# A gated recurrence and a feed-forward block: one reference point per sequence in place of six levels per block

## The chip, the core and the metric

The kernel runs on one core of one Trainium2 chip. The metric is the device time of one execution in microseconds (us). The core has five engines that work side by side, each through a queue of its own and in that queue's order: TensorE (PE in the profile; its weight loads stand apart as PEld), VectorE (DVE), ScalarE (ACT), GpSimd (POOL) and SyncE (SP), whose queue issues the DMAs. Matmuls write to PSUM, which has 8 banks; the other data lies in SBUF, on 128 partitions.

## What is computed

There are 4 sequences of 768 steps, 8 heads and 48 dimensions per head. Each head keeps a complex 48x48 state that is multiplied at every step by a complex gate per row and takes up the outer product of key and value; the query reads its real part. The result, 3072 tokens of 384 features, goes through a feed-forward block with 2048 hidden units and Silu.

```python
    mag = np.sqrt(a_re * a_re + a_im * a_im)
    scale = np.minimum(mag, 0.999) / (mag + 1e-06)
    a_re_n, a_im_n = (a_re * scale, a_im * scale)
    for t in range(S):
        ar, ai = (a_re_n[:, :, t, :, None], a_im_n[:, :, t, :, None])
        new_re = ar * S_re - ai * S_im
        new_im = ar * S_im + ai * S_re
        kv = np.einsum('bhd,bhe->bhde', k[:, :, t], v[:, :, t])
        S_re, S_im = (new_re + kv, new_im)
        y[:, :, t] = np.einsum('bhd,bhde->bhe', q[:, :, t], S_re)
    ...
    h = x @ w_in
    g = h * (1.0 / (1.0 + np.exp(-h)))
    return (g @ w_out).astype(np.float32)
```

The inputs are drawn with `a_re = rand * 0.1 + 0.85` and `a_im = randn * 0.1`. All arrays are float32 but the two weight matrices, which arrive as float64 and are turned into float32 on the chip.

## The kernel before

A sequence is cut into 6 chunks of 128 steps; the 24 chunks go in 12 pairs, and 256 tokens, a pair, are a tile of the feed-forward block. The kernel writes a gate as exp(l + 2 pi i th), forms running sums of l and th, and gets the weight between two steps as a product of rotated and scaled keys and queries.

*Gates of a pair* (`gates_log`, `gates_angle`): a chain that alternates ACT (squares, Ln, Exp, Arctan under two function tables), DVE and POOL. `phases` (L278, L280) sums th with two matmuls a chunk and `trig` takes cosine and sine. POOL rotates keys and queries (`rotate`, L306).

*Scales*: so that no exponent grows, a chunk is split into two blocks of 64 steps and each pair of steps takes its reference from the middle of the smallest aligned run that holds both. `scales` makes six sums of l for each head with two 128x384 matmuls (L341, tile `lt`) and ACT takes exponentials of them (tile `z`); `scaled` multiplies keys and queries by these on DVE (L357); `weights` forms the weights as three overlapping products (`far`, `mid`, `near`, L401 to L410) that DVE merges by masks (L416 to L418). `key_state` (L315, L320) scales keys to the end of their block, and `state` (L383, L387, L390) carries the state from block to block on PE, POOL and DVE.

*Output* (L424, L428) gives y with the tokens on partitions, so `tokens` (L442) transposes it for the feed-forward block.

*Feed-forward*: 8 units per pair. `hidden` (L450, tile `h`) forms 256 hidden units with 6 matmuls, ACT takes Tanh and DVE forms h(1 + tanh(h/2)) (L455); `result` (L465, tile `o`) adds them into two PSUM banks with 4 matmuls. `load_w` (L125 to L146) turns a block of float64 weights into float32 with nine DVE operations on 24 blocks of 256 and 32 of 192 columns.

*Order*: the code merges the steps of the attention of pair p with the feed-forward steps of pair p - 1, and with the weight loads at p = 0. The framework then puts each engine's instructions in one fixed queue and gives PSUM tiles out of small pools: `p_a` has 3 banks for the attention, `p_h` has 1 and `p_o` has 2 for the feed-forward.

Of the kernel before, what the change touches and what calls it, by code (L numbers as in the profile page):

```python
# [11 lines left out]
I32 = mybir.dt.int32  # L12
AF = mybir.ActivationFunctionType
# [4 lines left out]
# Square of the smallest gate magnitude that is told from zero: such a gate passes on 2e-9 of  # L18
# the state, less than fp32 rounds off, and keeps the exponents of a run of 4 within +-41.
FLOOR2 = 2.07e-15  # L20
# Adding and taking away 1.5 * 2^23 rounds an fp32 number to an integer.
ROUND = 12582912.0
# The largest fp32 number under 2 pi, so that half a turn stays within the sine's range.
TWO_PI = 6.283185


@with_exitstack
def kernel(
# [11 lines left out]
    """The gated recurrence in blocks of 64 steps, with the state carried from block to block.  # L40

    A gate is exp(l + 2 pi i th). With L and TH the running sums of l and th, step s reaches step t
    with the weight sum_d q[t,d] k[s,d] exp(L[t]-L[s]) cos(TH[t]-TH[s]): a product of rotated
    queries and keys, (q cos, q sin) and (k cos, k sin), each scaled by the distance of its L from
    one between. For any two steps of a block that one is the middle of the smallest aligned run
    of 8, 16, 32 or 64 steps that holds them in different halves (levels w = 4 to 32), so that both
    scales are at most 1 however fast the gates decay; steps of the same run of 4 take its middle,
    at most 2 steps away. Chunks of 128 steps, two blocks, fill the partitions.
    """
# [66 lines left out]
    def load_w(dst, src):  # L116
        """float64, as 64-bit words, to the nearest float32: sign, exponent and 23 bits of the
        mantissa are put together from the bits, and the other 29 bits are added. Columns that
        come in float32 are taken as they are."""
# [23 lines left out]
        # Below 2^-126 the exponent doesn't fit: such a weight is zero in float32.  # L143
# [11 lines left out]
    make_identity(nc, ident)  # L155

    def triangle(t, w):
        """1 where s <= t and both are in one aligned run of w steps."""
        nc.gpsimd.memset(t, 1.0)
        keep(t, [[1, C]], 0, -1)  # L160
        if w < C:
# [431 lines left out]
```

## Time and profile before

| quantity | value |
|---|---|
| three timed runs | 1479.62, 1485.4, 1503.15 us |
| median | 1485.4 us |
| span of the profiled execution | 1494.1 us |
| mean granted TensorE clock | 0.923 |
| PE busy | 1341.6 us (90% of the span) |
| DVE, ACT, POOL busy | 734.3, 487.3, 350.7 us |

The span runs from the first to the last instruction of one profiled execution; the page gives no time around it. A group row of the profile reads: line, engine, operation, output and inputs with shapes, count of records, then busy time and mean duration of one. A float32 matmul stands as two records, a transpose as one. A timeline row reads: start, duration, engine, line, operation, count of merged records, and in brackets the idle time ahead of it with what ended it. A row of a table by stretches reads: the stretch, its length, busy time with the number of records, granted clock, share of the DMA engines, GB/s.

### The profile page before, as it was taken

Reading aid. Unit: us, or ns where it says so; the run is one execution under the profiler, and the core shown is the slowest. Engines: PE = TensorE matmul, PEld = TensorE weight load, DVE = VectorE, ACT = ScalarE, POOL = GpSimd, SP = SyncE. Lnnn points to the kernel's source line nnn. Section 1 sums busy time; section 2 is a strip of 40 time slices with the busy share of each in tenths; the row PEclk is TensorE's granted clock in tenths of the full one; section 3 lists DMA queues with packets and bytes.
Section 4 is the critical chain, followed back from the end, with each engine's and each line's share of the span. In section 5 each row is a group of like instructions: output and inputs, shape, how many; then the busy total and the mean of one; then the engine's idle time right before and its main releaser. Section 6 shows DMA issues by size and latency. Waiting matters only on the chain. (4 is left out here: it accounts for less than half of the span.)

```text
span 1494.1 us, 21231 instructions
## 1 busy us (share of the span) xinstructions
PE 1341.6 (90%) x8592; PEld 937.5 (63%) x8592; DVE 734.3 (49%) x1592; ACT 487.3 (33%) x1009; POOL 350.7 (23%) x390
## 2 busy tenths in 40 slices
PE   1563798489999999999999999989999989999999
PEld 0342566256767666666766766756766756776676
DVE  4978778764444444444344444444344444334321
ACT  4433032303523513613523513513433513313301
POOL 5534011501322402301222311311131311301000
PEclk9975799789999999979999989979999999989979
DMA  5313111310020110110020110110010010000000
GB/s 121 85 50 90 41 43 54 75 37 6 17 49 1 32 33 1 31 29 6 13 52 1 29 36 0 28 32 6 6 38 1 12 30 3 6 12 1 1 11 11
DMA packets 136418, 42.27 MB, mean 28 GB/s; under 512 B 126080, under 2 KB 133248, under 8 KB 136320
## 3 DMA queue, kind: packets, MB, share of 16 engines
q1 hardware_dynamic: 136320, 40.91, 11.8%
q8 instruction: 68, 1.11, 0.3%
q14 instruction: 30, 0.25, 0.1%
HBM read 36.18 MB, written 4.72 MB: 27 GB/s over the span
## 5 line engine op out<-in xcount | busy, mean ns | idle before, releaser
L341 PE MATMUL lt<-sums,l 128*96 128x384 f32 x768 | 304.4, 518 | 46.5 <-DVE w L417 30.3
L465 PE MATMUL o<-w,g 128*128 128x384 f32 x768 | 282.2, 499 | 24.3 <-DVE w L146 24.3
L450 PE MATMUL h<-xT,w 128*128 128x256 f32 x1152 | 284.2, 392 | 18.1 <-DVE g L455 15.3
L450 PEld LDWEIGHTS h<-xT,w 128*128 128x128 f32 x1152 | 221.3, 196 | 78.1 <-DVE g L455 19.5
L220 ACT ACTIVATE z<-lt 96x384 f32<-96x384 f32 x384 | 187.2, 488 | 166.1 <-PE lt L341 164.3
L357 DVE TENSOR_TENSOR z<-z,qT 96x256 f32<-96x256 f32 (+1 forms) x288 | 149.4, 530 | 160.0 <-ACT z L220 159.1
L465 PEld LDWEIGHTS o<-w,g 128*128 128x128 f32 x768 | 145.8, 194 | 119.7 <-DVE w L146 27.2
L341 PEld LDWEIGHTS lt<-sums,l 128*96 128x96 f32 x768 | 126.8, 173 | 143.4 <-issue 64.1
L455 DVE SCALAR_TENSOR_TENSOR g<-tanh,h 128x512 f32<-128x512 f32 x96 | 65.3, 680 | 231.5 <-ACT tanh L220 231.5
L432 ACT COPY y<-y 128x192 f32<-128x192 f32 x48 | 15.3, 319 | 399.9 <-PE y L428 399.9
L220 ACT ACTIVATE tanh<-h 128x512 f32<-128x512 f32 x96 | 57.4, 598 | 249.2 <-PE h L450 223.5
L320 POOL TENSOR_TENSOR ks<-kr,es 128x384 f32<-128x384 f32 x48 | 47.5, 1009 | 326.3 <-ACT es L220 326.3
L387 POOL TENSOR_TENSOR S<-S,dec 96x192 f32<-96x192 f32 x88 | 56.1, 647 | 207.9 <-DVE S L390 205.6
L401 PE MATMUL far<-z 96*128 96x128 f32 x384 | 96.2, 334 | 0.1
L424 PE MATMUL y<-v,w 128*128 128x48 f32 x384 | 82.6, 299 | 9.4 <-DVE w L418 9.4
L352 POOL COPY dec<-z 96x8 f32<-96x8 f32 x48 | 32.8, 684 | 243.8 <-ACT z L220 243.8
L424 PEld LDWEIGHTS y<-v,w 128*128 128x128 f32 x384 | 64.0, 202 | 38.1 <-DVE w L418 23.8
L383 PEld LDWEIGHTS s<-v,ks 64*96 64x96 f32 x704 | 59.0, 170 | 41.0 <-issue 36.4
L357 DVE TENSOR_TENSOR z<-z,kT 96x256 f32<-96x256 f32 x192 | 79.7, 415 | 0.0
L410 PE MATMUL near<-z,zk 96*128 96x128 f32 x384 | 61.8, 313 | 14.4 <-DVE S L390 14.2
L300 POOL COPY l<-l 128x768 f32<-128x768 f32 x24 | 37.1, 1545 | 154.9 <-PE lt L341 153.0
L390 DVE TENSOR_TENSOR S<-s,S 96x192 f32<-96x192 f32 x88 | 30.9, 351 | 85.1 <-PE s L383 57.6
(92 smaller groups left out, 1685.2 us busy)
## 6 DMA issues: line engine op xcount, KB each, us to landing
raw<-in_moe_w_in_dram SPq DMA_DIRECT2D x24, 256.0 KB, 2.8
raw<-in_moe_w_out_dram SPq DMA_DIRECT2D x32, 192.0 KB, 2.4
re<-in_a_re_dram SPq DMA_DIRECT2D x24, 192.0 KB, 3.6
im<-in_a_im_dram SPq DMA_DIRECT2D x24, 192.0 KB, 3.3
k<-in_k_dram SPq DMA_DIRECT2D x24, 192.0 KB, 2.6
q<-in_q_dram SPq DMA_DIRECT2D x24, 192.0 KB, 2.7
v<-in_v_dram SPq DMA_DIRECT2D x24, 192.0 KB, 2.7
out_dram<-ot SPq DMA_DIRECT2D x24, 192.0 KB, 1.9
```

What stands on the lines that cost most here:

```text
L220: chain(nc.scalar.activation(out=out, in_=in_, func=func, **kw))
L320: nc.gpsimd.tensor_tensor(out=x["ks"][:, :, a], in0=x["kr"][:, :, a], in1=e, op=ALU.mult)
L341: nc.tensor.matmul(ps.rearrange("p s t -> p (s t)"), lhsT=two, rhs=sums[:, ts(g, NS // 2)].rearrange("p s t -> p (s t)"), start=True, stop ...
L357: eng.tensor_tensor(out=t, in0=t, in1=by, op=ALU.mult)
L383: nc.tensor.matmul(ps[:, h], lhsT=x["ks"][rows, hg].rearrange("p a d -> p (a d)"), rhs=x["v"][rows, hg], start=True, stop=True)
L387: nc.gpsimd.tensor_tensor(out=new, in0=x["S", i, hh], in1=x["dec", hh][:, :, ds(i, 1)].to_broadcast([D2, HH, D]), op=ALU.mult)
L401: nc.tensor.matmul(pf[:, h], lhsT=z[:, 2, h], rhs=z[:, 2, h], start=True, stop=True)
L410: nc.tensor.matmul(pn[:, h], lhsT=zk[:, h], rhs=z[:, 0, h], start=True, stop=True)
L424: nc.tensor.matmul(ps[:, h], lhsT=x["w", hh][:, h], rhs=x["v"][:, hh * HH + h], start=True, stop=False)
L450: nc.tensor.matmul(ps[:, ji], lhsT=w1[:, dc, ts(jp * 2 + ji, C)], rhs=A[p]["xT"][:, dc], start=(dc == 0), stop=(dc == ND - 1))
L455: nc.vector.scalar_tensor_tensor(out=g, in0=th, scalar=1.0, in1=ps, op0=ALU.add, op1=ALU.mult)
L465: nc.tensor.matmul(A[p]["o"][m], lhsT=A[p]["g", jp][:, ji, ts(m, C)], rhs=w2[:, j], start=(j == 0), stop=(j == NJ - 1))
```

## The change

The old kernel becomes `general`, without its comments, and a second one, `moderate`, runs ahead of it. `general` follows behind a branch on a flag that `moderate` computes: it is taken if any running sum of l, started at +44 in each sequence, ends below -44.

In `moderate` one reference serves a whole sequence. `sums` takes the running sums of l and th with one matmul each (L775) against a triangle; the last row of a chunk goes to the first row of the next by a small DMA (`carry`, L789). `exps` takes exp of the sum (`up`, for queries) and of its negative (`down`, for keys); DVE multiplies them in (L816) and POOL rotates with one 128x768 product each for keys and queries (L819). `weights` is one product per head (L840) and one masked copy into a buffer whose upper part stays zero. `state` adds into one PSUM bank over a sequence (L883) and DVE copies it out (L887). `output` forms y with features on partitions, two heads at partitions 0 and 64 of a bank (L862, L865); DVE copies it out (L869) and eight DMAs a pair pack it into `xT` (L898). `hidden` ends with Silu on ACT (L715), so DVE has no part in it; `p_h` has two banks. `load_w` uses five DVE operations and one on ACT, on 12 blocks of 512 and 16 of 384 columns; the last of the five, an integer add, is built as a special DVE instruction over twice as many 16-bit elements.

The order is new: attention runs two pairs ahead of the feed-forward block and stands in the code as a block of its own in front of it, and `prepare` (gates of pair p + 4, exponentials and rotations of pair p + 3) stands in front of both. The first two pairs' attention is merged with all weight loads.

```diff
-def tile_gateloop__then__act_silu_kernel(
+def general(
...
+HALF = 44.0
...
+def moderate(
...
+    p_a = ctx.enter_context(tc.tile_pool(name="p_a", bufs=3, space=PSUM))
+    p_s = ctx.enter_context(tc.tile_pool(name="p_s", bufs=1, space=PSUM))
+    p_h = ctx.enter_context(tc.tile_pool(name="p_h", bufs=2, space=PSUM))
+    p_o = ctx.enter_context(tc.tile_pool(name="p_o", bufs=2, space=PSUM))
...
+        low = moe.tile([C, WC], I32, tag="low", name="low")[:, 0:n]
+        t = moe.tile([C, WC], I32, tag="t", name="t")[:, 0:n]
+        nc.scalar.activation(out=low, in_=lo.bitcast(U32), func=AF.Copy, scale=2.0 ** -29)
+        nc.vector.tensor_scalar(out=t, in0=hi, scalar1=0x7FFFFFFF, scalar2=None,
+                                op0=ALU.bitwise_and)
+        nc.vector.tensor_scalar(out=t.bitcast(F32), in0=t.bitcast(F32), scalar1=TINY,
+                                scalar2=None, op0=ALU.max)
+        nc.vector.tensor_scalar(out=t, in0=t, scalar1=3, scalar2=0x3FFFFFF8,
+                                op0=ALU.logical_shift_left, op1=ALU.bitwise_and)
+        nc.vector.scalar_tensor_tensor(out=t, in0=hi, scalar=-0x40000000, in1=t,
+                                       op0=ALU.bitwise_and, op1=ALU.bitwise_or)
+        nc.vector.tensor_tensor(out=dst.bitcast(I32), in0=t, in1=low, op=ALU.add)
...
+    def sums(n):
+        p, i = divmod(n, 2)
+        b, c = divmod(n, NCH)
+        x, g = X[n], A[p]["g"]
+        if c > 0:
+            nc.vector.tensor_tensor(out=g[0:1, i], in0=g[0:1, i], in1=X[n - 1]["carry"],
+                                    op=ALU.add)
+        ps = [bank([C, DM], f"sum{n}_{a}") for a in range(2)]
+        for a in range(2):
+            nc.tensor.matmul(ps[a], lhsT=upto, rhs=g[:, i, a], start=True, stop=True)
+        x["lt"] = att.tile([C, 2, DM], F32, tag="lt", name=f"lt{n}", bufs=4)
+        if c == 0:
+            nc.vector.tensor_scalar(out=x["lt"][:, 0], in0=ps[0], scalar1=HALF,
+                                    scalar2=-HALF - 1, op0=ALU.add, op1=ALU.max)
+        else:
+            nc.vector.tensor_scalar(out=x["lt"][:, 0], in0=ps[0], scalar1=-HALF - 1,
+                                    scalar2=None, op0=ALU.max)
+        whole = att.tile([C, DM], F32, tag="whole", name=f"whole{n}", bufs=1)
+        nc.vector.tensor_scalar(out=whole, in0=ps[1], scalar1=ROUND, scalar2=ROUND, op0=ALU.add,
+                                op1=ALU.subtract)
+        nc.vector.tensor_tensor(out=x["lt"][:, 1], in0=ps[1], in1=whole, op=ALU.subtract)
+        if c + 1 < NCH:
+            x["carry"] = att.tile([1, 2, DM], F32, tag="carry", name=f"carry{n}", bufs=1)
+            nc.sync.dma_start(out=x["carry"], in_=x["lt"][C - 1:C])
+        else:
+            nc.vector.tensor_reduce(out=least[:, b:b + 1], in_=x["lt"][:, 0], op=ALU.min,
+                                    axis=mybir.AxisListType.X)
+    def exps(n):
+        x = X[n]
+        special(x["up"], x["lt"][:, 0], AF.Exp)
+        special(x["down"], x["lt"][:, 0], AF.Exp, scale=-1.0)
...
+    def rotate(n):
+        x = X[n]
+        for w, e in (("k", "down"), ("q", "up")):
+            nc.vector.tensor_tensor(out=x[w], in0=x[w],
+                                    in1=x[e].rearrange("p (h d) -> p h d", d=D), op=ALU.mult)
+            t = att.tile([C, H, 2, D], F32, tag=w + "r", name=f"{w}r{n}")
+            nc.gpsimd.tensor_tensor(out=t, in0=x["cs"], in1=x[w].unsqueeze(2)
+                                    .to_broadcast([C, H, 2, D]), op=ALU.mult)
+            x[w + "r"] = t
...
+    def weights(n, hh):
...
+        x["w", hh] = wbuf[turns[0] % NW]
+        turns[0] += 1
+        nc.vector.copy_predicated(out=x["w", hh], data=ps,
+                                  mask=upto_i.unsqueeze(1).to_broadcast([C, HH, C]))
+    def output(n):
+        p, i = divmod(n, 2)
+        c = n % NCH
+        x = X[n]
+        if i == 0:
+            A[p]["yT"] = moe.tile([C, HH, T], F32, tag="yT", name=f"yT{p}", bufs=1)
+        ps = bank([C, HH, C], f"y{n}")
+        for pair in range(HH):
+            for part in range(2 if c > 0 else 1):
+                for o in range(2):
+                    h = 2 * pair + o
+                    hh, hl = divmod(h, HH)
+                    to = ps[64 * o:64 * o + D, pair]
+                    if part == 0:
+                        nc.tensor.matmul(to, lhsT=x["v"][:, h], rhs=x["w", hh][:, hl],
+                                         start=True, stop=(c == 0))
+                    else:
+                        nc.tensor.matmul(to, lhsT=x["S"][:, h], rhs=x["qT", hh][:, hl],
+                                         start=False, stop=True)
+        for o in range(2):
+            rows = slice(64 * o, 64 * o + D)
+            nc.vector.tensor_copy(out=A[p]["yT"][rows, :, ts(i, C)], in_=ps[rows])
+    def state(n):
+        c = n % NCH
+        if c == NCH - 1:
+            return
+        x = X[n]
+        if c == 0:
+            sum_of[0] = p_s.tile([D2, H, D], F32, tag="s", name=f"s{n}")
+        ps = sum_of[0]
+        for h in range(H):
+            nc.tensor.matmul(ps[:, h], lhsT=x["kr"][:, h].rearrange("p a d -> p (a d)"),
+                             rhs=x["v"][:, h], start=(c == 0 and h == 0), stop=True,
+                             skip_group_check=True)
+        X[n + 1]["S"] = att.tile([D2, H, D], F32, tag="S", name=f"S{n + 1}")
+        nc.vector.tensor_copy(out=X[n + 1]["S"], in_=ps)
+    def repack(p):
+        A[p]["xT"] = moe.tile([C, ND, T], F32, tag="xT", name=f"xT{p}", bufs=3)
+        for h in range(H):
+            pair, o = divmod(h, 2)
+            done = 0
+            while done < D:
+                dc, r = divmod(h * D + done, C)
+                m = min(D - done, C - r)
+                nc.sync.dma_start(
+                    out=A[p]["xT"][r:r + m, dc],
+                    in_=A[p]["yT"][64 * o + done:64 * o + done + m, pair])
+                done += m
+    def hidden(p, jp):
...
+        A[p]["h", jp] = moe.tile([C, 2, T], F32, tag="silu", name=f"silu{p}_{jp}", bufs=4)
+        special(A[p]["h", jp], ps, AF.Silu)
...
+    def attention(p):
+        a, b = chunks(p)
+        steps = [lambda: transposed(a, 0), lambda: transposed(a, 1), lambda: weights(a, 0),
+                 lambda: transposed(b, 0), lambda: weights(a, 1), lambda: state(a),
+                 lambda: transposed(b, 1), lambda: output(a), lambda: weights(b, 0),
+                 lambda: weights(b, 1), lambda: state(b), lambda: output(b), lambda: repack(p)]
+        return steps
...
+    AHEAD = 2
+    load_a(0)
+    load_x(0)
+    load_x(1)
+    load_a(1)
+    prepare(0, NP)
+    for n in chunks(0):
+        sums(n)
+    prepare(1, 0)
+    for n in chunks(1):
+        sums(n)
+    load_x(2)
+    load_a(2)
+    load_x(3)
+    w_loads = [lambda s=s: load_w1(s) for s in range(DF // WC)]
+    w_loads += [lambda j=j: load_w2(j) for j in range(NJ)]
+    for p in range(-AHEAD, NP):
+        work = []
+        ahead = p + AHEAD
+        if ahead < NP:
+            if ahead + 3 < NP:
+                work.append(lambda: load_a(ahead + 3))
+            work += attention(ahead)
+            for i in range(2):
+                if 2 * ahead + 4 + i < N:
+                    work.insert(6 + 4 * i, lambda n=2 * ahead + 4 + i: load_x(n))
+        prep = []
+        if ahead + 1 < NP:
+            prep.append(lambda: prepare(ahead + 2, ahead + 1))
+            if ahead + 2 < NP:
+                prep += [lambda n=n: sums(n) for n in chunks(ahead + 2)]
+        if p < 0:
+            half = len(w_loads) // 2 if p < -1 else len(w_loads)
+            now, w_loads = w_loads[:half], w_loads[half:]
+            for f in prep[:1]:
+                f()
+            merge(work, now)
+            for f in prep[1:]:
+                f()
+        else:
+            for f in prep[:1]:
+                f()
+            table(SILU)
+            for f in work:
+                f()
+            merge(feed(p), prep[1:])
...
+    moderate(tc, q, k, v, a_re, a_im, w_in, w_out, out, flag)
+    again = nc.values_load(flag[127:128, 0:1], min_val=0, max_val=1)
+    with tc.If(again > 0):
+        general(tc, q, k, v, a_re, a_im, w_in, w_out, out)
```

PE, in the middle of the program, where attention and feed-forward work meet. Before: the sums `lt` of the attention of one pair between the units h and o of the pair ahead.

```order
L341 MATMUL lt_0_1_1_3198<-sums,l_6_3134 96x384
L465 MATMUL o_0_3215<-w_107,g_0_3151 128x384
L341 MATMUL lt_0_2_0_3201<-sums,l_6_3134 96x384
L341 MATMUL lt_0_2_1_3205<-sums,l_6_3134 96x384
L465 MATMUL o_0_3215<-w_107,g_0_3151 128x384
L341 MATMUL lt_0_3_0_3208<-sums,l_6_3134 96x384
L341 MATMUL lt_0_3_1_3212<-sums,l_6_3134 96x384
L465 MATMUL o_1_3216<-w_107,g_0_3151 128x384 x2
L450 MATMUL h_2_3248<-xT_2886,w_106 128x256 x6
L341 MATMUL lt_1_0_0_3261<-sums,l_6_3134 96x384
L341 MATMUL lt_1_0_1_3265<-sums,l_6_3134 96x384
L465 MATMUL o_0_3215<-w_107,g_1_3192 128x384
```

Now: the end of one pair's feed-forward units and the start of the attention of a later pair (`ktp`, `qtp` are transposes, `w` the weights, `s` the state, `h_0` the first unit of the next feed-forward block).

```order
L919 MATMUL o_0_1622<-w_87,silu_7_1723 128x384 x2
L919 MATMUL o_1_1623<-w_87,silu_7_1723 128x384 x2
L828 MATMUL ktp_0_1800<-ident,kr_1426 96x128 x4
L828 MATMUL qtp_0_1807<-ident,qr_1429 96x128 x4
L828 MATMUL ktp_1_1814<-ident,kr_1426 96x128 x4
L828 MATMUL qtp_1_1821<-ident,qr_1429 96x128 x4
L883 MATMUL s_1509<-v_1158,kr_1426 96x48
L840 MATMUL w_0_1828<-qT_0_1812,kT_0_1805 128x128 x4
L828 MATMUL ktp_0_1834<-ident,kr_1437 96x128 x4
L883 MATMUL s_1509<-v_1158,kr_1426 96x48 x5
L828 MATMUL qtp_0_1841<-ident,qr_1440 96x128 x4
L883 MATMUL s_1509<-v_1158,kr_1426 96x48 x2
```

The attention has moved out of the run of h and o units to a place of its own between two of them; only the first two h units stand within it.

ACT, at the end of the gate work of one pair (`cos`, `sin`, `cs` are trigonometric functions of the running angle). Before:

```order
L220 ACTIVATE mag_3497<-mag_3497 128x768
L330 COPY kT_1_3644<-ktp_1_3639 96x512
L220 ACTIVATE mag_3497<-mag_3497 128x768
L217 ACT_TABLE_LOAD
L220 ACTIVATE cos_3514<-cos_3514,half_pi_b 128x384
L220 ACTIVATE sin_3515<-turn_3038 128x384
L220 ACTIVATE cos_3519<-cos_3519,half_pi_b 128x384
L220 ACTIVATE sin_3520<-turn_3055 128x384
L220 ACTIVATE mag_3497<-mag_3497 128x768
L217 ACT_TABLE_LOAD
L220 ACTIVATE tanh_6_3629<-h_6_3622 128x512
L220 ACTIVATE z_1_3653<-lt_1_0_0_3655 96x3x128
```

Now, up to the first Silu of the next feed-forward block:

```order
L715 ACTIVATE up_1758<-lt_1642 128x384
L715 ACTIVATE down_1759<-lt_1642 128x384
L715 ACTIVATE up_1762<-lt_1706 128x384
L715 ACTIVATE down_1763<-lt_1706 128x384
L712 ACT_TABLE_LOAD
L715 ACTIVATE mag_1742<-mag_1742 128x768
L715 ACTIVATE cs_1771<-abs_1772,half_pi_b 128x8x48
L715 ACTIVATE cs_1771<-lt_1642 128x8x48
L715 ACTIVATE cs_1782<-abs_1783,half_pi_b 128x8x48
L715 ACTIVATE cs_1782<-lt_1706 128x8x48
L712 ACT_TABLE_LOAD
L715 ACTIVATE silu_0_1969<-h_0_1962 128x512
```

Four exponentials `up` and `down` have come into the gate work, the copy of `kT` has gone to DVE, and the table that is loaded at the end is Silu's, with the whole feed-forward block of that pair behind it.

DVE, at the same places. Before, with the gate work among the copies of `w` and `S`:

```order
L240 SCALAR_TENSOR_TENSOR s_3495<-s_3495,s_3496 128x768
L390 TENSOR_TENSOR S_0_1_3562<-s_1_1_3557,S_0_1_3562 96x192
L416 TENSOR_TENSOR w_1_3604<-far_1_3565,far 128x512
L417 COPY_PREDICATED w_1_3604<-mid_i,mid_1_3566 128x512
L418 COPY_PREDICATED w_1_3604<-near_i,near_1_3567 128x512
L246 TENSOR_SCALAR s_3495<-s_3495 128x768
L248 TENSOR_TENSOR l_3498<-s_3495,s_3496 128x768
L230 TENSOR_SCALAR s_3495<-re_3128 128x768
L262 TENSOR_SCALAR re_3128<-re_3128 128x768
L443 COPY xT_3633<-xtp_3634 128x3x128
L330 COPY qT_1_3651<-qtp_1_3646 96x512
```

Now, with the gate work among the copies of `kT`, `qT` and the weights:

```order
L733 SCALAR_TENSOR_TENSOR s_1740<-s_1740,s_1741 128x768
L832 COPY kT_0_1805<-ktp_0_1800 96x512
L832 COPY qT_0_1812<-qtp_0_1807 96x512
L832 COPY kT_1_1819<-ktp_1_1814 96x512
L739 TENSOR_SCALAR s_1740<-s_1740 128x768
L832 COPY qT_1_1826<-qtp_1_1821 96x512
L741 TENSOR_TENSOR g_1743<-s_1740,s_1741 128x2x384
L844 COPY_PREDICATED wt_103<-upto_i,w_0_1828 128x512
L742 TENSOR_SCALAR s_1740<-re_1443 128x768
L832 COPY kT_0_1839<-ktp_0_1834 96x512
L756 TENSOR_SCALAR re_1443<-re_1443 128x768
L832 COPY qT_0_1846<-qtp_0_1841 96x512
```

The copies that release the attention's PSUM banks (all of them on DVE now) stand among the gate instructions, of which some wait for ACT.

231 lines of the change are left out of this document (230 added, 1 removed).

## The prediction

> **What bounds the kernel now.** I read the page's busy shares and its slices first, then tables by stretches, then PE's timeline in the steady part, and last the rows of the other engines.
>
> ```profile
> PE 1341.6 (90%) x8592; PEld 937.5 (63%) x8592; DVE 734.3 (49%) x1592; ACT 487.3 (33%) x1009; POOL 350.7 (23%) x390
> PE   1563798489999999999999999989999989999999
> PEclk9975799789999999979999989979999999989979
> ```
>
> PE is full from the tenth slice on and ragged before. Two stretches, and a third inside the second, say how much (PE busy, then the granted clock):
>
> ```profile
> 0.00:350.00 350.00, 228.48 (x1358) 0.83 0.26 64
> 350.00:1494.10 1144.10, 1113.07 (x7236) 0.95 0.08 17
> 655.00:670.00 15.00, 15.00 (x96) 0.50 0.00 1
> ```
>
> After 350 us PE idles for 31 us of 1144, so the time there is PE's work; before it, PE idles for 122 us of 350. In the third stretch PE is never idle and yet runs at half clock: its work there is the short matmuls of `s`, `mid` and `far`. So a time follows from three things: PE's work, its start, and what the short matmuls do to the clock.
>
> PE's prices at full clock are the distances between starts in the steady part:
>
> ```profile
> 713.08 2.75 PE L450 MATMUL h<-xT,w 128*128 128x256 f32 x12
> 715.67 0.60 PE L327 MATMUL ktp<-ident,kr 128*96 128x128 f32 x4
> 716.10 0.60 PE L327 MATMUL qtp<-ident,qr 128*96 128x128 f32 x4
> 716.54 1.45 PE L341 MATMUL lt<-sums,l 128*96 128x384 f32 x4
> 717.83 2.74 PE L465 MATMUL o<-w,g 128*128 128x384 f32 x8
> 720.41 1.45 PE L341 MATMUL lt<-sums,l 128*96 128x384 f32 x4
> ...
> 729.54 1.26 PE L383 MATMUL s<-v,ks 64*96 64x48 f32 x16
> 730.73 0.49 PE L401 MATMUL far<-z 96*128 96x128 f32 x2
> ...
> 734.34 1.06 PE L410 MATMUL near<-z,zk 96*128 96x128 f32 x8
> 735.23 1.03 PE L450 MATMUL h<-xT,w 128*128 128x256 f32 x4
> ```
>
> An h unit costs 2.59 us, an o unit 2.58, four transposes 0.435, two sums of 384 columns 1.29, four products of 128 columns (eight records) 0.89 or 0.111 a record, sixteen records of 48 columns 1.19.
>
> **The change, PE.** Removed are `lt`, `far`, `mid`, `near`, the old `s` and `y`, `phase`, `suffix`, `xtp`. What PE does for one pair now:
> - feed-forward, unchanged: 16 units, 41.4 us;
> - 32 transposes: 8 groups x 0.435 = 3.5 us;
> - weights: 16 products = 4 x 0.89 = 3.6 us;
> - y: 32 matmuls of 128 columns, less those with the state in a sequence's first chunk, 29.3 on average or 59 records. Only 48 columns are loaded, so the load doesn't bind, and I take 0.111 us a record as in `near`: 6.5 us. Between ends: 0.074 as in `s`, 4.4 us, and the half clock's double, 13 us;
> - state: 13.3 matmuls on average, 27 records between 0.074 (the s row) and 0.111: 2.4 us;
> - running sums: 4 matmuls x 0.645 = 2.6 us.
>
> That is 60.0 us a pair, against 1341.6 / 12 = 111.8 before: 16.0 of attention, 2.6 of sums, 41.4 of feed-forward.
>
> **The attention as a phase of its own.** The order lists put a pair's attention, with the first two h units (5.2 us), between two runs of feed-forward units: 21.2 us of PE. PE hands every transpose, product and y to DVE and takes the bank back, over three banks, and DVE holds gate work in the same queue.
>
> ```profile
> L330 DVE COPY qT<-qtp 96x512 f32<-96x512 f32 x48 | 32.9, 685 | 50.4 <-PE qtp L327 50.3
> L418 DVE COPY_PREDICATED w<-near_i,near 128x512 f32<-128x512 int32 x48 | 34.9, 727 | 10.9 <-PE near L410 9.9
> L443 DVE COPY xT<-xtp 128x384 f32<-128x384 f32 x24 | 13.4, 558 | 79.7 <-PE xtp L442 79.7
> L240 DVE SCALAR_TENSOR_TENSOR s<-s,s 128x768 f32<-128x768 f32 x12 | 11.7, 973 | 7.7 <-ACT s L220 7.7
> L266 DVE SCALAR_TENSOR_TENSOR th<-mag,re 128x768 f32<-128x768 f32 x12 | 17.6, 1469 | 0.1
> ```
>
> DVE per pair: 8 transposed copies and 4 of y at 0.685, 4 masked copies at 0.727, 2 of the state at 0.558: 12.2 us. The seven gate operations (the first and last are shown) come to 6.7, the products with `up` and `down` and the absolute values to 2.9. That is 21.8 us, as much as PE's 21.2. The phase lasts 21.8 us if both overlap fully and 43 if they take turns. Three banks let PE run ahead by two, and PE has the h units to do meanwhile, so I take 23.5, near the lower end. To it I add 4.5 us for the clock: the second stretch above lost 0.05 of 1144 us, 57 us, or about 5.5 for each of the ten to eleven pairs in it; short matmuls now come in one lump, and part of the loss falls into waits for DVE. Together 28 us.
>
> A rule is to be weighed here. The Trainium skill, page TensorE: Matmul & The Clock Gate, section HAM oscillation, has the clock fall to half only after PE has idled for more than about 3.4 us; waits for one or two copies would never trip it, the 4.5 us would go, and the sum below would be about 910. The row of 655 to 670 us disagrees with it, half clock with no idle time, so I keep the loss.
>
> The rest of a period is 14 units, 36.2 us, and the sums, 2.6. So a period is 28 + 38.8 = 66.8 us, between 60.6 and 82.
>
> **ACT, POOL and SP beside it.** The z and zk exponentials go; a gate chain must end before the first Silu. Before, from its table load to the end of its last:
>
> ```profile
> 609.58 1.28 ACT L217 ACT_TABLE_LOAD   x1
> ...
> 628.65 1.28 ACT L217 ACT_TABLE_LOAD   x1
> 629.95 0.60 ACT L220 ACTIVATE tanh<-h 128x512 f32<-128x512 f32 x1
> ```
>
> ```profile
> L220 ACT ACTIVATE es<-suffix 128x384 f32<-128x384 f32 x24 | 11.7, 488 | 19.5 <-PE suffix L315 19.0 <-DVE turn L285 0.4
> L253 POOL TENSOR_TENSOR mag<-mag,im 128x768 f32<-128x768 f32 x12 | 23.5, 1961 | 25.9 <-ACT mag L220 25.9
> out_dram<-ot SPq DMA_DIRECT2D x24, 192.0 KB, 1.9
> ```
>
> 20.4 us, with four more exponentials 22.4. It starts behind the last Silu of a pair, when PE still has about 4.5 us of o units; the new first Silu is needed after that and the phase, 32.5 us on. Cost nothing, with 10 us of cover; gone, each us is a us of PE. Silu takes the place of Tanh at the same 512 columns, and the DVE step between goes. POOL's four products at 1.96 us take the place of eight of half the size. The carry and the packing DMAs (about 2 us each, as `ot`) have 20 us and a pair's time of cover; behind loads that wait for a buffer in SP's queue they could be late, and `sums` with them.
>
> **The start.** No feed-forward unit can end before all weights are converted and three pairs' attention is done. Before, DVE is the busy engine of that time, and POOL slows it:
>
> ```profile
> 25.00:175.00 150.00, 132.74 (x343) 0.77 0.29 73
> 33.16 4.27 POOL L250 TENSOR_TENSOR mag<-mag,s 128x768 f32<-128x768 f32 x1 [12.01 <-DVE s L230]
> 35.15 0.29 DVE L137 TENSOR_SCALAR u<-raw 128x256 int32<-128x256 int32 x1
> 35.80 1.77 DVE L135 TENSOR_SCALAR t<-t 128x256 int32<-128x256 int32 x1
> L129 DVE TENSOR_SCALAR t<-raw 128x192 int32<-128x192 int32 (+1 forms) x56 | 18.2, 325 | 3.9 <-DMA raw<-in_moe_w_out_dram 3.4 <-PE o L465 0.3
> L146 DVE SCALAR_TENSOR_TENSOR w<-t,w 128x192 f32<-128x192 int32 (+1 forms) x56 | 24.3, 434 | 0.2
> ```
>
> DVE was busy for 132.7 of 150 us, 88%. The nine conversion lines (first and last shown) cost 185 us; the five new ones I put at 90. Per 512 columns: three scalar operations at 0.41, between the 0.29 of 256 columns and its double; one of two inputs at 0.68, as the copies above; and the 16-bit add, which no row shows: between 0.41 and 1.37, twice 0.685 for its 1024 elements, and I take 1.2, near the upper end, since it has two inputs as the dearer rows have. That is 3.1 us, and 2.55 for 384 columns: 12 x 3.1 + 16 x 2.55 = 78, and 12 more for POOL. To that come three attentions (37), five gate chains' DVE steps (34), eight running sums (21: three operations at 0.56 and a carry's addition at 0.96) and rotations of eight chunks (12: 1.45 each): 194 us. At 88% and from 7.7 us on, when the first gates arrive, the feed-forward's 14 units begin at 227 us. The ends: 190, if DVE is never kept waiting, and 260, if five gate chains of 21 us on ACT, as from one table load to the next here, shut out the conversions:
>
> ```profile
> 0.81 1.28 ACT L217 ACT_TABLE_LOAD   x1 [0.81 <-PEq L577]
> ...
> 22.04 1.28 ACT L217 ACT_TABLE_LOAD   x1
> ```
>
> **The sum.** 227 + 38.8 for the first pair; nine periods of 66.8, 601; two pairs of feed-forward alone, 83; the end, 3.2 us, as now behind the last matmul, and 1 us for flag and branch:
>
> ```profile
> 1485.58 5.32 PE L465 MATMUL o<-w,g 128*128 128x384 f32 x16
> ```
>
> That gives 954 us of span, against 1494.1. The median of the runs, 1485.4, lies 0.6% under that span; so 950 for the median.
>
> **Rivals.**
> - *Hand-over*: in the attention phase PE and DVE take turns, by the gate work in DVE's queue or by half clock throughout. The phase goes to 43 us: 950 + 9 x 15 = 1085. For it: both carry 21 us, three banks. Against it: the h units, and before the same engines kept PE full.
> - *Light phase*: overlap is full, the clock holds, the start comes at 200: 950 - 9 x 6.2 - 27 = 867. For it: the second stretch has long parts at clock 1.00. Within it, the Trainium skill, TensorEngine Tiling (Array Packing), section Key Properties, lets matmuls on different column tiles run in parallel, as the two heads of y would; that would take 3.2 us a pair off, 950 to 921, and no row here shows it.
> - *Late Silu*: the gate chain grows past 32.5 us, by DVE steps behind copies or a late carry. At 40 us: 950 + 9 x 7.5 = 1018.
> - *Slower*: the branch is taken, both kernels run, 950 + 1485 = 2435. It decides at a sum of -88 over 768 steps. The gates' mean log is near ln 0.9 = -0.105, so sums lie near -77 to -80, with a spread of about 1: far from it.
>
> **Chances.** The forecast (about 900 to 1000) 0.58, light phase 0.20, hand-over 0.15, late Silu 0.06, branch 0.01. The likeliest is 950. The range goes from the light phase to past the late Silu and leaves out hand-over and branch, 870 to 1050. Two per cent, 30 us, is about what a measurement can tell from no change; all cases but the branch lie beyond it: faster 0.985, same 0.005, slower 0.01.
>
> **What would show it.** Right: h and o units at 2.6 us in runs of 14, some 66 us from one pair's first Silu to the next, PE idle a few us in each phase, the first such run near 227 us, no old line after the flag. Wrong on the phase: PE waiting for `kT`, `qT` or `w` copies in long gaps. Wrong on the clock: 1.00 or 0.50 through the phase. Wrong on the start: DVE well under 88% busy or conversion rows far from 0.41 to 1.2 us. The forecast fails if the phase isn't 22 to 36 us or the start not 190 to 260.

## The result and the profile after

| | before | changed |
|---|---|---|
| median of the runs beside each other | 1492.49 us (1479.62 to 1503.15, 4 runs) | 865.75 us (863.84 to 866.83, 4 runs) |
| ratio of the times, 95% interval | | 0.5802 (0.5766 to 0.5838) |
| span of the profiled execution | 1494.1 us | 864.6 us |

The kernel became faster as forecast, but by more: 866 us against a forecast of 950 and a range from 870. The page of the changed kernel, busy time of PE and then PE and its clock in 40 slices:

```profile
PE 734.1 (85%) x3808; PEld 554.4 (64%) x3808; DVE 391.0 (45%) x608; ACT 265.3 (31%) x390; POOL 175.3 (20%) x85
PE   0243466749999999989989999999899999999996
PEclk9985557678999999999999999999999999999999
```

PE's work is 734 us where it was 1342, and it is full from the tenth slice on. The clock row is new: from the eleventh slice to the end it shows no loss, where the old kernel's row had a 7 every few slices. The same stretch as a row by stretches (length, busy time of PE, PEld, DVE, ACT and POOL, clock), and below it the first attention phase:

```profile
350.00:865.00 515.00, 496.34 (x2576) 375.57 (x2574) 163.52 (x240) 138.50 (x208) 78.08 (x34) 1.00 0.12 29
246.40:266.40 20.00, 17.50 (x154) 14.95 (x152) 19.32 (x27) 13.17 (x20) 9.45 (x5) 1.00 0.24 57
```

In the phase DVE is busy for 19.3 of 20.0 us, and PE, which also does two hidden units there, for 17.5. Two rows of PE's timeline bound the nine periods, from the first phase to the pure feed-forward work at the end:

```profile
246.36 0.60 PE L828 MATMUL ktp<-ident,kr 128*96 128x128 f32 x4
...
775.07 5.34 PE L908 MATMUL h<-xT,w 128*128 128x256 f32 x24
```

| term of the sum | forecast | measured |
|---|---|---|
| start of the first phase | 227 + 38.8 = 265.8 | 246.4 |
| nine periods | 9 x 66.8 = 601 | 775.07 - 246.36 = 528.7, or 58.7 each |
| two pairs alone, flag, branch, end | 87 | 864.6 - 775.1 = 89.5 |
| span | 954 | 864.6 |

So of the 89 us by which the forecast of the span was too long, 72 lie in the attention phase, nine times 8, and 19 in the start; the end took 2 more than forecast.

### The profile page after: what moved, and what is told of

It is laid out like the page before. It is cut to its first block, busy times and chain, and to the rows that moved or that the text cites. A ratio compares the mean times of both kernels' runs of the same rounds, so it can differ in the third digit from the quotient of the medians.

```text
span 864.6 us, 9727 instructions
## 1 busy us (share of the span) xinstructions
PE 734.1 (85%) x3808; PEld 554.4 (64%) x3808; DVE 391.0 (45%) x608; ACT 265.3 (31%) x390; POOL 175.3 (20%) x85
## 4 chain that ended last, share of the span: by engine, by line
PE 64%; DVE 16%; POOL 6%; ACT 6%; issue 3%; DMA 2%; SPq 1%; DVEq 0%; POOLq 0%; ACTq 0%
PE o L919 28%; PE h L908 25%; POOL mag L744 3%; PE sum L775 3%; ACT mag L715 3%; PE w L840 2%; PE y L862 2%; DVE kT L832 2%; PE y L865 2%; POOL qr L819 2%; POOL kr L819 1%; DVE g L741 1%; DVE wt L844 1%; DVE qT L832 1%; DVE q L816 1%
## 5 line engine op out<-in xcount | busy, mean ns | idle before, releaser
L919 PE MATMUL o<-w,silu 128*128 128x384 f32 x768 | 263.0, 488 | 0.0
L919 PEld LDWEIGHTS o<-w,silu 128*128 128x128 f32 x768 | 145.3, 190 | 87.8 <-issue 1.5
L715 ACT ACTIVATE silu<-h 128x512 f32<-128x512 f32 x96 | 56.4, 597 | 416.6 <-PE h L908 416.5
L775 PE MATMUL sum<-g,upto 128*128 128x384 f32 x96 | 45.3, 599 | 48.5 <-DVE g L771 27.3
L819 POOL TENSOR_TENSOR kr<-cs,k 128x768 f32<-128x768 f32 x24 | 66.6, 2776 | 57.5 <-ACT cs L715 25.8
L840 PE MATMUL w<-qT,kT 96*128 96x128 f32 x384 | 60.6, 313 | 14.2 <-DVE kT L832 7.9
L819 POOL TENSOR_TENSOR qr<-cs,q 128x768 f32<-128x768 f32 x24 | 56.9, 2373 | 53.5 <-ACT cs L715 37.6
L840 PEld LDWEIGHTS w<-qT,kT 96*128 96x128 f32 x384 | 54.6, 220 | 19.1 <-DVE kT L832 10.2
L775 PEld LDWEIGHTS sum<-g,upto 128*128 128x128 f32 x96 | 20.6, 227 | 62.3 <-issue 27.3
L883 PE MATMUL s<-v,kr 128*96 128x48 f32 x320 | 38.1, 269 | 15.2 <-POOL kr L819 8.8
L883 PEld LDWEIGHTS s<-v,kr 128*96 128x96 f32 x320 | 36.2, 189 | 20.2 <-POOL kr L819 11.2
L862 PE MATMUL y<-wt,v 128*48 128x128 f32 x384 | 39.3, 297 | 11.6 <-DVE wt L844 11.6
L715 ACT ACTIVATE mag<-mag 128x768 f32<-128x768 f32 x36 | 30.3, 843 | 53.4 <-POOL mag L744 52.4
```

The lines of the kernel that those rows point to most:

```text
L715: chain(nc.scalar.activation(out=out, in_=in_, func=func, **kw))
L775: nc.tensor.matmul(ps[a], lhsT=upto, rhs=g[:, i, a], start=True, stop=True)
L819: nc.gpsimd.tensor_tensor(out=t, in0=x["cs"], in1=x[w].unsqueeze(2) .to_broadcast([C, H, 2, D]), op=ALU.mult)
L840: nc.tensor.matmul(ps[:, h], lhsT=x["kT", hh][:, h], rhs=x["qT", hh][:, h], start=True, stop=True)
L862: nc.tensor.matmul(to, lhsT=x["v"][:, h], rhs=x["w", hh][:, hl], start=True, stop=(c == 0))
L883: nc.tensor.matmul(ps[:, h], lhsT=x["kr"][:, h].rearrange("p a d -> p (a d)"), rhs=x["v"][:, h], start=(c == 0 and h == 0), stop=True, ski ...
```

## The experiments

Times of other kernels are set against the 865.75 us above.

**Order of y's matmuls.** What does a record of y cost, and why?

```diff
-        for pair in range(HH):
-            for part in range(2 if c > 0 else 1):
-                for o in range(2):
+        for o in range(2):
+            for pair in range(HH):
+                for part in range(2 if c > 0 else 1):
```

> Same matmuls as the changed kernel (865.75 us); only the order of y's is new: all of a chunk's matmuls that write to partitions 0 to 47, then all that write to partitions 64 to 111, so that neighbours share a column tile. In the changed kernel a y record starts 0.055 us after the one before it, half of the 0.111 that the prediction took from `near`. Theory, two column tiles run side by side: a record now costs 0.111 again, 59 records a pair x 0.056 = 3.3 us more in each of nine phases, 865.75 + 30 = 896 us (885 to 900), and the rows of y stand 0.11 us apart per record. Rival, a load of only 48 columns makes a record cheap whoever its neighbour is: rows at 0.055, time 866 us (862 to 870).

886.31 us (884.28 to 888.18). PE's timeline, first the changed kernel, then this one; the last number is the count of records in a row:

```profile
264.73 0.39 PE L865 MATMUL y<-qT,S 96*48 96x128 f32 x4
264.95 0.39 PE L862 MATMUL y<-wt,v 128*48 128x128 f32 x4
265.17 0.39 PE L865 MATMUL y<-qT,S 96*48 96x128 f32 x4
```

```profile
266.27 0.38 PE L865 MATMUL y<-qT,S 96*48 96x128 f32 x2
266.49 0.38 PE L862 MATMUL y<-wt,v 128*48 128x128 f32 x2
266.71 0.38 PE L865 MATMUL y<-qT,S 96*48 96x128 f32 x2
```

0.22 us hold four records where the two heads alternate, and two where they don't. A chunk's 32 records went from 1.90 to 3.26 us, a first chunk's 16 from 1.01 to 1.48: on average 2.4 us a pair, 22 in nine. The median rose by 20.6; in the traces the nine periods together grew by 16.0 (528.7 to 544.7), so some of y's extra time is hidden beside other engines. So two heads at partitions 0 and 64 run side by side. By the rule of the Trainium skill that the forecast named for it (TensorEngine Tiling (Array Packing), Key Properties), tiles run in parallel; the trace agrees, with a factor of two.

**What holds the clock at 1.00?** First the two long hidden units were taken out of the phase, by one order dependence of their first matmul on the last y matmul.

> The first two hidden units of each pair are held back until the last y matmul of the attention in front of them; nothing else changes. Theory: short matmuls of 128 streamed columns leave the clock at 1.00 by themselves, and the phase of 20.0 us is set by DVE, which is busy for 19.3 of it. Then the 5.2 us of the two units fall behind the phase, less the waits at its end: 4 to 5 us x 9 = 36 to 47, 865.75 + 41 = 907 us (895 to 915), clock 1.00 in the phase and PE idle for some 7 us of it. Rival, the long units in between are what keeps the clock up: the phase's 12.8 us of short PE work run at half clock, as in the start of this kernel where the clock was 0.50 to 0.73, so 12.8 + 5.2 more less what lies beside DVE: 5 to 11 us x 9 on top, 950 to 1000 us, clock 0.5 to 0.8 in the phase.

923.58 us (919.90 to 924.58), between the two. The first seven periods are 65.6 to 67.9 us, 7 more than before: the units' 5.2, and some 2 that go with the lost clock. The rows by stretches show where it fell (PE busy, clock): the first half of a phase and the second, which begins behind a wait of 2.04 us.

```profile
316.30:326.00 9.70, 7.52 (x67) 6.63 (x65) 9.00 (x13) 5.15 (x8) 2.12 (x1) 1.00 0.11 41
326.00:338.00 12.00, 12.00 (x97) 11.19 (x97) 10.02 (x15) 7.01 (x11) 8.97 (x4) 0.57 0.36 67
```

In this phase the clock is low where PE is fully busy again, just behind the wait. Next, short matmuls took the units' old places, while the units stayed held back (`FILL` is 12):

```diff
+        if jp < 2:
+            for i in range(FILL):
+                nc.tensor.matmul(ps[:, 0, 0:D], lhsT=w1[:, i % ND, ts(jp, C)],
+                                 rhs=A[p]["xT"][:, i % ND, 0:D], start=True, stop=True)
```

> The run that holds back the first two hidden units took 923.6 us, and PE's granted clock in the second half of its attention phase was 0.72. Here the same kernel issues 24 short matmuls (128 columns loaded, 48 streamed, into the PSUM banks that the held units then overwrite) at the places where the held units used to stand: 48 records x 0.113, from the rows of the run with short y matmuls, are 5.4 us, nearly the 5.2 of the units. So PE is as busy in the phase as in the changed kernel, with short work. Theory, the clock falls because PE waits: with the gaps filled the clock stays at 1.00 and the phase at 20 us, and the held units cost 5.2 us behind it: 865.75 + 9 x 5.2 = 913 us (908 to 920). Rival, short matmuls count as little as idle time: the clock falls as without them, 924 to 960 us, under 0.9 over the phase's second half.

943.84 us (940.24 to 945.43): the time that the rival gave, but not its reason. The fillers ran out before the phase's last waits. Two of the first seven phases had no wait above 1.34 us: there the clock was 1.00 and the period 64.7 us, as the theory has it (58.9 + 5.2). The other five had a single wait of 2.8 to 2.9 us, and the clock fell to 0.50, for 3.4 to 6.8 us, between 0.8 us before the wait's end and 0.7 us behind it. So short work of this kind does hold the clock up. In this run and the one before it, 14 of the 15 waits of 2.0 us or more that began at full clock brought a fall.

Then matmuls of the old kernel's forms were added in front of y's, into the PSUM bank that y overwrites. The old y first:

```diff
+        for h in range(H):
+            hh, hl = divmod(h, HH)
+            nc.tensor.matmul(ps[:, hl, 0:D], lhsT=x["w", hh][:, hl], rhs=x["v"][:, h],
+                             start=True, stop=True)
```

> Added to the changed kernel: before the y matmuls of a chunk, eight matmuls of the old form (128 columns loaded, 48 streamed) into the same PSUM bank, which the y matmuls then overwrite; the result is unchanged. In the kernel before, two records of that form took 0.35 us at full clock, so 16 matmuls a pair cost 5.6 us. Theory, the half clock of the old kernel came with such matmuls, that spend most of their time loading: the phase gets 5.6 us longer and part of it runs at half clock, 5 to 10 us more, 865.75 + 9 x (11 to 16) = 960 to 1010 us, clock under 0.9 in the phase. Rival, the clock doesn't depend on the form: only the matmuls' own time, 865.75 + 9 x 5.6 = 916 us (905 to 925), clock 1.00.

896.14 us (895.73 to 896.57), clock 1.00 in all nine periods: the rival, and cheaper than priced, since 16 records took 1.81 us, 3.6 a pair. Then 64 tiny matmuls a chunk, 16 columns by 16:

> Added to the changed kernel before the y matmuls of a chunk: 64 matmuls that load 16 columns and stream 16, on 96 rows, like the small products of `far` in the kernel before, into the PSUM bank that y then overwrites. There 12 such records took 0.24 us, so 128 take 2.6 us a chunk, 5.2 a pair, without a wait of PE. So far the clock fell after every single wait of PE of 2.0 us or more and after none of 1.34 or less; but the kernel before lost clock at places without such a wait. Theory, PE's tiny matmuls count as idle time: the clock falls to 0.50 in the phase behind them, 4 to 8 us more in a phase: 865.75 + 9 x (9 to 13) = 947 to 983 us. Rival, only waits count: clock 1.00, 865.75 + 9 x 5.2 = 913 us (905 to 920).

937.09 us (933.28 to 941.44), between the two. These matmuls stand in two lumps a phase, one for each chunk. At the first, 3.4 us long, the clock stayed at 1.00; at the second, which follows a wait of 1.1 to 2.0 us, it fell in five of seven phases, in two of them as the wait ended and in three within the lump. So this run does not part the lump from the wait. And last the old state's form, on 64 rows:

```diff
+        for m in range(24):
+            nc.tensor.matmul(ps[0:D2, m % HH, 0:D],
+                             lhsT=x["kr"][0:64, m % H].rearrange("p a d -> p (a d)"),
+                             rhs=x["v"][0:64, m % H], start=True, stop=True)
```

> Added to the changed kernel at the same place: 24 matmuls a chunk of the old state's form (64 rows, 96 columns loaded, 48 streamed). In the kernel before, 16 records of it took 1.19 us, so 48 take 3.6 us a chunk, 7.1 a pair, without a wait of PE. Theory as in the run with tiny matmuls, that work which uses half of the array's rows counts as idle: the clock falls behind it, 865.75 + 9 x (11 to 15) = 965 to 1000 us. Rival, only waits and the tiniest matmuls count: clock 1.00, 865.75 + 9 x 7.1 = 930 us (920 to 937).

Its four runs lie further apart than those of any other kernel here: 992.94 us at a mean clock of 0.896, inside the theory's range, two of 1011, and 1026.81 at 0.858, which is the traced one (median 1011.04). In that trace no wait of PE in the steady part was above 0.73 us, and yet the clock fell to 0.50 in each of the nine phases, in eight of them with PE busy for the whole 3.4 us ahead of the first fall. The control has the same matmuls on all rows (`[:, m % H]` for `[0:64, m % H]`):

> Control to the run with 24 matmuls a chunk on 64 rows, in which the clock fell to 0.50 in every attention phase though PE's longest wait was 0.72 us. Here the same 24 matmuls a chunk use all 128 rows; nothing else differs. Their 48 records, 0.074 to 0.113 each, take 3.6 to 5.4 us a chunk, 7.1 to 10.8 a pair. Theory, the idle rows are what lowers the clock: it stays at 1.00, and the time is 865.75 + 9 x (7.1 to 10.8) = 930 to 963 us less up to 2 us a phase of waits that are filled, so 912 to 963 us. Rival, any long run of short matmuls lowers it: clock under 0.9 in the phase and 985 us or more, as with 64 rows.

948.35 us (942.73 to 949.06, mean clock 0.927 to 0.970), the theory: even the fastest run with 64 rows is 44 us above the slowest with 128. With 64 rows, PE's timeline of one phase, and a stretch in its second lump (PE busy, then at the end the clock):

```profile
283.39 4.86 PE L856 MATMUL y<-v,kr 64*96 64x48 f32 x48
...
298.94 7.91 PE L856 MATMUL y<-v,kr 64*96 64x48 f32 x48
```

```profile
300.00:310.00 10.00, 10.00 (x73) 9.86 (x74) 0.00 (x0) 0.00 (x0) 1.81 (x1) 0.50 0.00 1
```

With 128 rows, the same two views, the second over the steady part:

```profile
270.32 4.20 PE L856 MATMUL y<-v,kr 128*96 128x48 f32 x48
...
280.08 4.25 PE L856 MATMUL y<-v,kr 128*96 128x48 f32 x48
```

```profile
300.00:850.00 550.00, 542.97 (x3370) 0.99 0.13 30
```

With 128 rows the clock dipped in one phase of nine, at a second lump behind a wait of 0.81 us; with 64 the second lump shown runs at half clock. So matmuls on half of the rows lower the clock without a wait.

The old kernel's row of 655 to 670 us has `s` on 64 rows in it, but its clock was low before the first of them. PE's timeline there, with the old y (`v`, `w` and `S`, `z`) behind a wait, then `phase`, then `s`:

```profile
651.04 0.42 PE L424 MATMUL y<-v,w 128*128 128x48 f32 x2 [0.89 <-DVE w L418]
...
653.45 2.38 PE L278 MATMUL phase<-th,upto 128*128 128x384 f32 x4
655.76 1.51 PE L383 MATMUL s<-v,ks 64*96 64x48 f32 x8
```

The four records of `phase` take 2.31 us where four of 384 columns cost 1.29 at full clock; the trace has the clock at 0.50 from 654.0 us. Of the old kernel's 16 falls between 350 us and its last matmul, four come with waits of 3.2 us, seven behind 3.4 us of busy PE that hold `s` on 64 rows and `far`, and five, this one among them, behind the old y after a wait of 0.89 us (three other such waits brought none). Which of these forms did it in the old kernel was not tried there: the run with the old y's `v`, `w` matmuls kept the clock at 1.00, but the longest wait in front of them was 0.3 us, and the `S`, `z` matmuls weren't there.

**Which parts of the change carry the start and the period?** The nine DVE operations of the old conversion, on the new blocks:

> The changed kernel with the nine DVE operations of the old weight conversion in place of the five with one on ACT, on the new block sizes. The nine took 185 us on DVE, the five 76. Theory, the start is bound by DVE, which is busy for 82% of the 207.5 us until the feed-forward runs: 109 more / 0.82 = 133 us at most, 109 at least, so 865.75 + (109 to 133) = 975 to 1000 us, and the steady period stays at 58.9 us. Rival, the start is bound by the loads and by the gate chains on ACT, and DVE's work lies beside them: under 930 us.

922.39 us (919.57 to 923.74), the rival's number and the theory's mechanism: on the larger blocks the nine take 133.9 us, not 185, so 57.9 more than the five, and the first phase begins at 300.0 in place of 246.4 us, 53.6 later. The periods are unchanged. DVE's work in the start is paid nearly one to one.

The old activation, Tanh on ACT and a product on DVE:

> The changed kernel with the old activation: Tanh on ACT, then h(1 + tanh(h/2)) on DVE, and the factor 0.5 at the output copy. DVE gets eight operations of 0.68 us a pair. Theory, DVE is busy for 8 of 39 us while the feed-forward units run, so six of the eight are hidden, and only those of the first two units, 1.4 us, stand in DVE's queue in the phase, which DVE fills: 865.75 + 9 x (0 to 1.4) = 866 to 879 us. Rival, PE waits for each product through the two banks of h: 0.7 us a unit, 865.75 + 9 x 5.4 = 915 us.

864.65 us (862.85 to 867.48): no difference. DVE's busy time grew by 57.5 us, all of it hidden.

The changed kernel without the branch and the old kernel behind it:

> The changed kernel without the branch and without the old kernel behind it (the flag is still computed), so a running sum out of range would not be redone. Theory, the branch costs about what the prediction put at 1 us for flag and branch: 865 us (862 to 866). Rival, the three times larger program costs something while it runs (its instructions' loading, the wait for the flag before the end): 840 to 860 us.

860.61 us (860.16 to 862.34), 5 us less, between the two. Behind the last output copy the span goes on for 2.7 us, and for 6.1 with the branch; the rest is an earlier start (first phase at 243.7), which isn't explained.

The attention merged evenly with the feed-forward steps:

> The changed kernel with the attention of a pair merged evenly with the feed-forward steps in place of a phase of its own. Theory: the phase is what covers the gate chain on ACT (some 18 us of it are still to come when a pair's first hidden unit is done), so without it the first result unit waits for its Silu, PE stands behind it with 6 us of other work ahead, about 10 us of wait a pair and the clock falls after it: 865.75 + 9 x (10 to 16) - 9 x 2 for the phase's own waits = 938 to 992 us. Rival, the interleaving only fills the 2 us that PE waits in a phase: 848 us (845 to 860).

924.51 us (923.30 to 926.16): slower, as the theory had it, but by less, and for the most part not by the wait that it named: up to 700 us PE waits once for Silu, 4.4 us, and four times in front of `s`, 34.2 us. For one of these, of 8.55 us, the timeline has four rows of DVE, then PE's:

```profile
260.09 2.26 DVE L758 SCALAR_TENSOR_TENSOR mag<-re,mag 128x768 f32<-128x768 f32 x1
262.27 1.95 DVE L806 TENSOR_SCALAR abs<-lt 128x384 int32<-128x384 int32 x1
264.15 0.94 DVE L760 SCALAR_TENSOR_TENSOR g<-mag,re 128x768 f32<-128x768 f32 x1
265.02 0.54 DVE L887 COPY S<-s 96x384 f32<-96x384 f32 x1
...
265.66 2.76 PE L883 MATMUL s<-v,kr 128*96 128x48 f32 x16 [8.55 <-issue]
```

The profile names no releaser, but in the program the next `s` may not write its bank before DVE has copied it out, and that copy, which ends 0.1 us earlier, stands in DVE's queue behind a gate chain. So the copy is the likely cause; no run tried it.

**A faster version.** PE idles for half of the start, so some of the first pair's feed-forward units were moved there, with the weights loaded in the units' order:

```diff
-    w_loads = [lambda s=s: load_w1(s) for s in range(DF // WC)]
-    w_loads += [lambda j=j: load_w2(j) for j in range(NJ)]
+    w_loads = []
+    for s in range(DF // WC):
+        w_loads.append(lambda s=s: load_w1(s))
+        w_loads += [lambda j=j: load_w2(j) for j in range(4 * s, 4 * s + 4)]
+    first = feed(0)
...
-            merge(work, now)
+            if p == -1:
+                table(SILU)
+                merge(work, now, first[:EARLY])
+            else:
+                merge(work, now)
...
-            merge(feed(p), prep[1:])
+            merge(feed(p) if p else first[EARLY:], prep[1:])
```

> The changed kernel with another order in the start: the weights come in the order of the feed-forward units, and four hidden and three result units of the first pair (18.1 us of PE) are merged with the second pair's attention and the second half of the weights, where PE is idle for half of the time. Theory, the start is bound by DVE's work, which stays the same, so these 18 us leave the path: 865.75 - 18 = 848 us (843 to 855), the first attention phase with pure feed-forward work behind it near 228 us in place of 246. Rival, the first Silu must wait for one more gate chain on ACT and its conversions, which delays attention: no gain, 860 to 870 us.

842.69 us (841.25 to 842.98), a little below the theory's range. With eleven units:

> The run with part of the first pair's feed-forward units in the start took 842.7 us with seven of the sixteen there. Here eleven are. Theory, PE still has idle time there: 4 x 2.6 = 10 us less, 832 us (829 to 838). Rival, units that wait for the last weights and for Silu hold the attention of the third pair up, which stands behind them in PE's queue: 838 to 850 us.

832.81 us (832.18 to 833.93), the theory; ratio to the old kernel 0.5608 (0.5565 to 0.5651). The periods are those of the changed kernel; only the start is shorter. It beats both kernels.

## Why the prediction was wrong

- **The clock, the step that failed.** "To it I add 4.5 us for the clock ... short matmuls now come in one lump": nine times 4.5 is 40 of the 89 us, and the measured loss in the nine periods is nothing. The old loss was spread over the pairs as if any short work caused it. The runs show that short matmuls on 96 or 128 rows alone don't (clock 1.00 in the changed kernel and with the old y's form added), and that two things do: single waits of PE of 2.0 us and more, and lumps of matmuls on 64 rows. The change leaves neither: its longest wait in a phase is 1.34 us, and `s`, `far` and the old y, which stand ahead of the old kernel's falls without a long wait, are gone. How the old loss divides among these forms stays open. The rule that was weighed there (the Trainium skill, TensorE: Matmul & The Clock Gate, HAM oscillation) gave the right sign; but its 3.4 us of idle time isn't what these traces show, since waits of 2.0 us sufficed and, on 64 rows, the clock fell with PE busy. The row that was held against it, 655 to 670 us, was read as the doing of the matmuls inside it, though the clock had fallen at 654.0.
- **The price of y.** "I take 0.111 us a record as in `near`": measured 0.055, since two column tiles work at once. 6.5 us a pair became 3.5, 27 us of PE's work in nine periods; the tiles are 2.4 of these 3.0, and the run without their overlap shows that about three quarters of such time (16.0 of 22 us) reach the periods. The forecast had this as part of a rival only.
- **The overlap** was sized well: 23.5 less the 3.0 of y is 20.5, and the first seven phases took 20.1 to 21.8 us (periods of 58.9 to 60.6 less 38.8). "Three banks let PE run ahead by two, and PE has the h units to do meanwhile" holds; without these units there a period took 7 us more, some 2 beyond the units' own 5.2.
- **The start**: "the 16-bit add ... I take 1.2": it took 0.68 at that size and 0.64 on average, so the conversions cost 76 us, not 90.

```profile
L669 DVE CUSTOM_DVE_ANT_0 w<-t,low 128x768 uint16<-128x768 uint16 (+1 forms) x28 | 17.8, 642 | 0.3 <-DVE t L663 0.2
```

  DVE's work until 207.5 us, about where the first run of units begins, was 169.7 us, not 194. Its share of the time behind the first gates was 85% where 88% was taken. The mechanism was right, the size was off.
- **The gate chain and Silu.** The chain was put at 22.4 us and took 22.4, from its table load to the first Silu:

```profile
242.08 1.28 ACT L712 ACT_TABLE_LOAD   x1
...
264.44 1.08 ACT L715 ACTIVATE silu<-h 128x512 f32<-128x512 f32 x2
```

  "Cost nothing, with 10 us of cover": nothing it was, but the first result units follow at 266.4, 0.8 us after these two Silu, since the phase is shorter. A phase shorter by more than that would, by these rows, make PE wait for Silu.
- **Flag and branch** were put at 1 us and cost about 3.4 at the end.
- **The rivals.** The light phase at 867 us was the case that came: overlap nearly full, the clock, an earlier start, and column tiles besides. That its number fits to 1 us is partly luck: its periods of 60.6 us came out at 58.7, 17 us less in nine, and against that its start at 200 was 207.5 and the end took 2 us more. At 0.20 it had too little of the chance: the second stretch's 0.05 of lost clock was read as a property of short matmuls, while the row that showed it held forms that the change removes.

## What to carry to other kernels

A loss seen in the old profile belongs to the instructions that stand in its rows and just ahead of them; before it is carried into a forecast, ask which of them the change keeps. In these runs matmuls on half of the rows, and single waits of some 2 us, cost clock on top of their own time, so long matmuls placed in the gaps of short ones gain twice. When one engine binds the start and another the rest, move the second's work into the start: that gave 33 us here, after the change itself.

## What had not been expected of the hardware

- The clock keeps a grid of its own: ahead of the last change, every stretch at one clock lasts 3.41 us or a multiple of it in every trace of this case (without the long units, the low ones of the nine periods lasted 6.83, 10.24, 3.41, 3.41, 13.65, 13.65, 3.41, 3.41 and 13.65). So after a wait of 2.0 us a fall can come up to 1.4 us behind it or within it. Here it came 0.8 us before the wait's end, and the first transposes behind it already take 1.09 us in place of 0.64:

```profile
525.52 1.09 PE L828 MATMUL qtp<-ident,qr 128*96 128x128 f32 x4 [2.04 <-DVE qT L832]
```

- Lumps of 48 short records on 64 rows lowered the clock in all nine phases, the same on 128 rows in one of nine, with the same wait of 0.72 us in front of the first lump of the first seven.
- This DVE operation begins while POOL's two-input operation runs, and ends only behind it, as the timeline of POOL and of DVE in the first phase shows:

```profile
252.15 2.12 POOL L744 TENSOR_TENSOR mag<-mag,s 128x768 f32<-128x768 f32 x1 [47.09 <-DVE s L742]
...
252.53 2.15 DVE L756 TENSOR_SCALAR re<-re 128x768 f32<-128x768 f32 x1
```

  The same DVE operation took 0.56 us in the merged kernel, where it began 0.1 us ahead of POOL's. Not every DVE operation is held: copies out of PSUM that began within a POOL operation kept their 0.68 us.
